# Feed-forward by halves of 288 tokens, outputs turned by DMA, products in token order: a change to a fused attention and feed-forward kernel

## Chip, cores and metric

The kernel runs on one core of one Trainium2 chip. The metric is the device time of one execution in microseconds (us), lower is better. Runs are compared in the same state of the chip and beside runs of the kernel before on the same chip; a run over 1.5% above the fastest of its kernel is called slow and left out of the ratios. "Span" is the time from the first to the last instruction in a profile; it is some 1.8 us shorter than the device time (256.4 against 258.15 us in the profile before).

## The reference

Eight batches of 576 tokens, eight heads of 64 channels. Heads 0 to 3 ("plain") look back over 32 tokens, heads 4 to 7 ("dilated") over 32 tokens in steps of 4. The concatenated heads go through a multiplicative feed-forward.

```python
def _attn_ref(q, k, v):                       # (8, 8, 576, 64)
    scores = scale * np.matmul(q, k.transpose(0, 1, 3, 2))
    rel = pos[:, None] - pos[None, :]
    mask_plain = (rel >= 0) & (rel < 32)
    mask_dil = (rel >= 0) & (rel < 128) & (rel % 4 == 0)
    ...                                       # softmax under the head's mask
    return np.matmul(attn, v)

def _moe_ref(x, w1, w2, w3, w_out):           # x: (4608, 512)
    h = (x @ w1) * (x @ w2) @ w3              # 1024 wide
    return h @ w_out                          # (4608, 512)
```

## The kernel before

TensorE does everything in one stream: `w3 @ w_out` is fused once into `wf_sb`; then each tile of 512 tokens gets its gated products (`ffn1`: two matrices of four matmuls of 512 columns per 128 of the 1024 channels, the first cast by ScalarE, the product by VectorE) and four results `y` (`ffn2`). The attention of later batches is put between these at counted "points". A batch's attention has four steps: two dilated halves (u = 1), then two plain halves (u = 0). A step is: scores (TensorE), exp (ScalarE), mask (VectorE), values (TensorE), reciprocal and normalise into `xo` (VectorE), and a turn of `xo` into channels, `XT`. In the kernel before, the turn is done on TensorE, but for the dilated halves of late batches, which a DMA turns.

```python
# self.by_dma = u == 1 and b > 1 and (b, hf) != (2, 1)
def to_channels(self, ps=ps_x, copy=None):
    if self.by_dma:
        for hp in range(2):
            nc.sync.dma_start(out=XT[:, 2 + hp, t0 : t0 + HALF]..., in_=self.xo[0:96, hp]..., transpose=True)
        return
    ...                       # six turns on TensorE into PSUM, one copy into XT

def ffn1(t, f, point):
    for i, w_sb in enumerate((w1_sb, w2_sb)):
        point()
        ps = bank()                                  # three banks in turn
        ffn1_half(t, f, w_sb, (2, 3, 0, 1), ps)      # four matmuls, 512 columns
        if i == 0: nc.scalar.copy(out=a_sb, in_=ps)
    nc.vector.tensor_tensor(out=gts[t][:, f], in0=pss[1], in1=a_sb, op=AL.mult)

for t in range(1, NT):
    for f in range(KFF): ffn1(t, f, point)
    for tb in range(4):  ffn2(t, tb, point)          # rows stored with a step of 4
```

Tokens stand in `XT` sorted by their number modulo 4, so `ffn2` stores rows with a step of four. Loads of q, k and v are issued by GpSimd two batches ahead, each as soon as its buffer is free.

The softmax here doesn't subtract the row's maximum and nothing guards it: scores larger than these inputs give would overflow.

Of the kernel before, what the change touches and what calls it, by code (L numbers as in the profile page):

```python
# [1 line left out]

# [29 lines left out]

SLOTS = (0, 2, 1, 3)


@with_exitstack
def kernel(
# [46 lines left out]
    XT = const.tile([P, DCH, n_tok], BF16, name="XT")  # L84
# [20 lines left out]
    def bank():  # L105
        return banks.tile([P, TB], F32, tag="f", name="f")
# [125 lines left out]
    def transpose_qk(b, u, which):  # L232


        src, dst = ((qn, qts), (kn, kts))[which]
        pad = PADK * which
        t = src[b][:, u, :].bitcast(U32).rearrange("p (a i) -> p a i", a=ROWS)
        o = dst[u][b % 2].rearrange("p s c -> p (s c)").bitcast(U32)[:, pad : pad + S]
        if u == 0 and which == 1:
            nc.vector.transpose(out=o.rearrange("p (j a) -> p a j", a=ROWS), in_=t)  # L240
            return
        for a0 in range(4):

            n = 5 - a0 // 2
            at = RES * SLOTS.index(a0)
            step = RES * SLOTS.index((a0 + 2) % 4) + (a0 + 18) // 4 - at
            nc.vector.transpose(  # L247
                out=bass.AP(
                    tensor=o.tensor,
                    offset=o.offset + at,  # L250
                    ap=[o.ap[0], [1, n], [9, 16], [step, 2]],
                ),
                in_=t[:, a0 : a0 + 4 * n - 3 : 4, :],
            )

    class Step:
        def __init__(self, n, b, u, hf):
            self.b, self.u, self.hf = b, u, hf
            self.et = ets[n % NET]

            self.by_dma = u == 1 and b > 1 and (b, hf) != (2, 1)
# [106 lines left out]
        def to_channels(self, ps=ps_x, copy=None):  # L368
            if self.by_dma:
                for hp in range(2):  # L370
                    t0 = self.b * S + HALF * self.hf
                    nc.sync.dma_start(
                        out=XT[:, 2 + hp, t0 : t0 + HALF].rearrange("p (m t) -> p m t", m=3),
# [4 lines left out]
            xv = ps[:, 0 : 2 * HALF].rearrange("p (h s t) -> p h s t", h=2, s=4)  # L378
            for hp in range(2):
                for m in range(3):  # L380
                    if self.u == 0:
                        xo = xv[:, hp, :, 24 * m : 24 * m + 24]
                    else:
                        xo = xv[:, hp].rearrange("p s t -> p (s t)")[:, 96 * m : 96 * m + 96]
                    nc.tensor.transpose(  # L385
                        out=xo,
# [3 lines left out]
            dst = XT[:, 2 * self.u : 2 * self.u + 2, self.b * S : (self.b + 1) * S]  # L390
            if self.u == 0:
                t0 = 72 * self.hf
                dst = dst.rearrange("p h (s t) -> p h s t", s=4)[:, :, :, t0 : t0 + 72]
            else:
                t0 = HALF * self.hf
                dst = dst[:, :, t0 : t0 + HALF].rearrange("p h (s t) -> p h s t", s=4)
            if copy is None:
                copy = nc.vector.tensor_copy if self.u == 0 and self.b > 1 else nc.scalar.copy
# [29 lines left out]
    def first_batch():  # L428
# [22 lines left out]
        ps_b = [pool.tile([P, TB], F32, name=f"ps_b{i}") for i in range(4)]  # L451
        begin(0, 0, ps_b[0])
        begin(0, 1, ps_b[1])
        p0.to_channels()
        begin(1, 0, ps_b[2])
        p1.to_channels(bank().bitcast(BF16), nc.vector.tensor_copy)
        begin(1, 1, ps_b[3])
# [33 lines left out]
    def segment(lo, hi):  # L491

        for i in range(lo, hi + 2):
            st = steps[i] if i < hi else None
            p1 = steps[i - 1] if lo <= i - 1 < hi else None
            p2 = steps[i - 2] if lo <= i - 2 else None
            at, b = i % 4, i // 4
            more = 4 * (b + 1) < hi and st is not None
            if st is not None:
                later(st.scores, after=1.0 if p2 is not None and not p2.by_dma else 1.6)  # L500
            if p2 is not None and not p2.by_dma:
                later(p2.to_channels)
                done_at[i - 2] = len(phases)
            if p1 is not None:
                later(p1.values, after=1.6)
                if p1.by_dma:
                    behind(p1.to_channels)
            if st is not None:
                if at == 0:
                    behind(transpose_qk, b, 0, 1)  # L510
                if at == 1:
                    if more:
                        behind(transpose_qk, b + 1, 1, 0)
                if at == 2:
                    behind(prefetch, b + 2)
                if at == 2 and more:
                    behind(transpose_qk, b + 1, 1, 1)
                if at == 3 and more:
                    behind(transpose_qk, b + 1, 0, 0)
# [5 lines left out]
    gts = {}  # L525

    def ffn1_half(t, f, w_sb, cs, ps):
        for c in cs:
            nc.tensor.matmul(  # L529
                out=ps,  # L530
                lhsT=w_sb[:, c, f * P : (f + 1) * P],
                rhs=XT[:, c, t * TB : (t + 1) * TB],
# [6 lines left out]
    def begin(f, i, ps):  # L539

        begun[f, i] = ps
        ffn1_half(0, f, (w1_sb, w2_sb)[i], (2, 3), begun[f, i])

    def ffn1(t, f, point):
        if t not in gts:
            gts[t] = wk_pool.tile([P, KFF, TB], BF16, tag="gt", bufs=3, name="gt")
        pss = []
        for i, w_sb in enumerate((w1_sb, w2_sb)):
            point()
# [168 lines left out]
```

## Time and profile before

| | before |
|---|---|
| time, median of 3 runs | 258.35 us (258.26 to 259.26) |
| span of the profile | 256.4 us |
| TensorE busy | 246.9 us (96%) |
| VectorE, ScalarE busy | 154.7, 111.2 us |
| turns on TensorE, turning DMAs | 126, 22 |

The page gives the busy time of each engine and the chain of work that ended last. The table of windows gives busy times by stretch, so that one sees where an engine idles. The groups give count, mean duration and what the engine waited for. The lines themselves stand in the prediction below, with what is to be seen in them.

### The profile page before, as it was taken

The page shows a single profiled execution, that of the slowest core. Times are in us where ns is not written, and L with a number is a line of the kernel's source. Part 1 is how long each engine was busy: PE and PEld are TensorE (multiplying, and loading weights), DVE is VectorE, ACT ScalarE, POOL GpSimd, SP SyncE. Part 2 cuts the span into 40 slices and gives each one's busy share as a digit, 9 for nine tenths or more (in the row PEclk, how much of TensorE's full clock was granted, in tenths as well). Part 3 has the DMA queues.
Part 4 walks back from the last instruction along what each step waited for, and adds up shares of the span by engine and source line. Part 5 has one row for each costly group of instructions (what it writes and reads, how often), then busy time and mean ns, then how long its engine had stood idle before and what let it go on. Part 6 is the DMA issues. An engine that isn't in the chain of part 4 may idle for free.

```text
span 256.4 us, 5585 instructions
## 1 busy us (share of the span) xinstructions
PE 246.9 (96%) x2281; PEld 124.7 (49%) x2318; DVE 154.7 (60%) x326; ACT 111.2 (43%) x161; POOL 57.7 (23%) x84
## 2 busy tenths in 40 slices
PE   7899999999999999999999999999999999999994
PEld 2454455655445544554455454545544544444443
DVE  6565445968897688848775777588746623412420
ACT  2444266554554454444445444444354224324232
POOL 8962235537261123114210600000000000000000
PEclk9999999999999999999999999999999999999999
DMA  6999999999999999686969791220142031014004
GB/s 102 167 189 208 207 212 200 190 197 213 247 188 176 211 201 139 96 157 149 115 107 211 107 92 42 98 76 3 48 100 66 0 92 74 0 51 113 3 27 137
DMA packets 59001, 32.12 MB, mean 125 GB/s; under 512 B 45024, under 2 KB 49376, under 8 KB 58976
## 3 DMA queue, kind: packets, MB, share of 16 engines
q0 software_dynamic: 46160, 20.70, 67.4%
q1 hardware_dynamic: 12816, 11.07, 15.8%
q8 instruction: 18, 0.29, 0.5%
q14 instruction: 7, 0.06, 0.1%
HBM read 41.39 MB, written 9.44 MB: 198 GB/s over the span
## 4 chain that ended last, share of the span: by engine, by line
PE 90%; DVE 3%; DMA 2%; issue 2%; ACT 1%; POOL 0%; POOLq 0%; ACTq 0%
PE f L529 45%; PE f L585 24%; PE f L615 5%; PE ps_a L319 4%; PE ps_a L277 4%; DMA kn<-in_k_dram 2%; PE ps_x L385 2%; PE ps_b L529 1%; PE f L601 1%; PE ps_s L277 1%; PE ps_s L293 1%; PE ps_x L179 1%; DVE xo L330 1%; DVE kt L240 0%; DVE gt L560 0%
## 5 line engine op out<-in xcount | busy, mean ns | idle before, releaser
L529 PE MATMUL f<-XT,w_sb 128*128 128x512 bf16 x537 | 127.0, 379 | 1.5 <-issue 0.5
L529 PEld LDWEIGHTS <-w_sb 128*128 128x128 bf16 x576 | 53.3, 98 | 60.2 <-DVE XT L399 0.6
L560 DVE TENSOR_TENSOR gt<-f,asb 128x512 bf16<-128x512 f32 x70 | 48.1, 687 | 38.5 <-PE f L529 37.8
L559 ACT CAST asb<-f 128x512 bf16<-128x512 f32 x70 | 41.0, 586 | 63.7 <-PE f L529 63.7
L585 PE MATMUL f<-wf_sb,gt 128*128 128x512 bf16 (+1 forms) x288 | 66.0, 373 | 1.0 <-issue 0.8
L592 ACT COPY osb<-f 128x512 f32<-128x512 f32 (+1 forms) x37 | 21.2, 574 | 47.5 <-PE f L585 47.2
L585 PEld LDWEIGHTS <-gt 128*128 128x128 bf16 x296 | 27.1, 98 | 27.9 <-DVE gt L560 0.5
L307 ACT ACTIVATE et<-ps_a 128x1152 bf16<-128x1152 f32 x28 | 31.7, 1134 | 7.9 <-PE ps_a L277 7.9
L140 POOL DMA_DIRECT2D vd<-in_v_dram x32 | 21.2, 668 | 39.8 <-PE ps_a L319 31.4
L330 DVE TENSOR_TENSOR xo<-ps_a,rcp 96x768 bf16<-96x768 f32 x28 | 26.7, 953 | 1.0
L247 DVE STREAM_TRANSPOSE qt<-qn 128x160 uint32<-128x160 uint32 (+1 forms) x64 | 19.6, 421 | 1.1 <-DMA qn<-in_q_dram 1.1
L308 DVE TENSOR_TENSOR et<-et,mask_di 128x1152 bf16<-128x1152 bf16 x14 | 10.6, 756 | 15.2 <-ACT et L307 15.2
L319 PEld LDWEIGHTS <-et 128*128 128x128 bf16 x384 | 15.8, 98 | 7.2 <-ACT et L297 0.6
L308 DVE TENSOR_TENSOR et<-et,mask_pl 128x1152 bf16<-128x1152 bf16 x14 | 10.6, 758 | 12.2 <-ACT et L307 12.0
L277 PEld LDWEIGHTS <-kt 32*128 32x128 bf16 x768 | 10.7, 92 | 14.7 <-issue 12.2
L615 PE MATMUL f<-wo_sb,w3T 128*128 128x512 bf16 x60 | 15.6, 379 | 0.2
L327 DVE RECIPROCAL rcp<-ps_a 96x12 f32<-96x12 f32 x28 | 6.2, 221 | 11.1 <-PE ps_a L319 11.0
L277 PE MATMUL ps_a<-qt,kt 32*128 32x96 bf16 x672 | 12.4, 202 | 0.1
L116 POOL DMA_DIRECT2D kn<-in_k_dram x10 | 6.4, 642 | 22.2 <-DVE kt L240 18.2
L116 POOL DMA_DIRECT2D qn<-in_q_dram x10 | 6.6, 662 | 18.8 <-DVE qt L247 15.3
L247 DVE STREAM_TRANSPOSE kt<-kn 128x160 uint32<-128x160 uint32 (+1 forms) x32 | 9.7, 416 | 1.6 <-DMA kn<-in_k_dram 1.5
L297 ACT ACTIVATE et<-ps_s 128x576 bf16<-128x576 f32 x8 | 5.2, 651 | 11.9 <-PE ps_s L277 11.6
(60 smaller groups left out, 142.9 us busy)
## 6 DMA issues: line engine op xcount, KB each, us to landing
qn<-in_q_dram POOLq DMA_DIRECT2D x6, 576.0 KB, 5.6
kn<-in_k_dram POOLq DMA_DIRECT2D x6, 576.0 KB, 9.4
w3n<-in_moe_w_dram POOLq DMA_DIRECT2D x4, 512.0 KB, 17.8
vp<-in_v_dram POOLq DMA_DIRECT2D x5, 384.0 KB, 7.0
out_dram<-osb SPq DMA_DIRECT2D x7, 256.0 KB, 2.3
out_dram<-osb SPq DMA_DIRECT2D x8, 224.0 KB, 2.3
out_dram<-osb SPq DMA_DIRECT2D x8, 192.0 KB, 3.0
out_dram<-osb SPq DMA_DIRECT2D x8, 160.0 KB, 3.0
```

Of the source, the lines that this page charges most:

```text
L140: nc.gpsimd.dma_start(out=vds[b % 2][p0 : p0 + n, 4 * m : 4 * m + 4, 16 : 16 + 2 * D], in_=bass.AP(tensor=x.tensor, offset=x.offset + (4 * ...
L247: nc.vector.transpose(out=bass.AP(tensor=o.tensor, offset=o.offset + at, ap=[o.ap[0], [1, n], [9, 16], [step, 2]],), in_=t[:, a0 : a0 + 4 ...
L277: nc.tensor.matmul(out=bank_of(h)[:, c0 : c0 + 96], lhsT=kt[prt, 96 * m : 96 * m + P, c], rhs=rhs, start=(start and c == 0), stop=(c == 1 ...
L307: nc.scalar.activation(out=ev, in_=ps_a[:, :, 0:HALF], func=ACT.Exp, scale=scale)
L308: nc.vector.tensor_tensor(out=ev, in0=ev, in1=mk.unsqueeze(1).to_broadcast([P, 4, HALF]), op=AL.mult)
L319: nc.tensor.matmul(out=out, lhsT=self.et[:, c0 : c0 + P], rhs=rhs, start=True, stop=True)
L330: nc.vector.tensor_tensor(out=xo[0:96].rearrange("p (n k) d -> p n k d", n=n), in0=ov[0:96, :, :, x0 : x0 + D], in1=rcp[0:96].unsqueeze(3) ...
L529: nc.tensor.matmul(out=ps, lhsT=w_sb[:, c, f * P : (f + 1) * P], rhs=XT[:, c, t * TB : (t + 1) * TB], start=(c == 2), stop=(c == 1),)
L559: nc.scalar.copy(out=a_sb, in_=ps)
L560: nc.vector.tensor_tensor(out=gts[t][:, f], in0=pss[1], in1=a_sb, op=AL.mult)
L585: nc.tensor.matmul(out=y, lhsT=gts[t][:, f, tb * P : (tb + 1) * P], rhs=wf_sb[:, f, c0 : c0 + n], start=(f == 0), stop=(f == KFF - 1),)
L615: nc.tensor.matmul(out=wf_ps[ft], lhsT=w3T[ft][:, g, :], rhs=wo_sb[:, g, :], start=(g == 0), stop=(g == KFF - 1),)
```

## The change

Its intent: turns cost TensorE time (43 ns each in the profile before, 126 of them), so from batch 2 on a DMA does them all. The feed-forward goes by halves of a batch (288 tokens), and results `y` of the half before are put between its products, to give ScalarE and VectorE time. Products are written to `gt` in token order, so that each tile of 128 tokens goes out in one plain store. A fourth PSUM bank (`ps_x`) joins the ring after batch 1; VectorE's turns of q and k are cut into pieces and spread.

```diff
-            self.by_dma = u == 1 and b > 1 and (b, hf) != (2, 1)
+            self.by_dma = b > 1
@@ bank()
+        if "x" in late:
+            late["x"] += 1
+            if late["x"] % 4 == 0:
+                return ps_x.bitcast(F32)
@@ ffn1
-        nc.vector.tensor_tensor(out=gts[t][:, f], in0=pss[1], in1=a_sb, op=AL.mult)
+        n0 = HALF * (2 * b + hf) % RING
+        g = gt[:, f, n0 : n0 + HALF].rearrange("p (i a c) -> p c a i", a=2, c=2)
+        pb, pa = (
+            x.rearrange("p (c a i) -> p c a i", c=2, a=2) for x in (pss[1], a_sb)
+        )
+        nc.vector.tensor_tensor(out=g, in0=pb, in1=pa, op=AL.mult)
@@ schedule
-    for t in range(2, 8):
-        marks.append((15 + 24 * t, done_at[4 * t + 3]))
+    for b in range(2, B):
+        marks.append((40 + 27.25 * (b - 1) - 4, done_at[4 * b + 3]))
@@ main loop
+    done, due = len(due), []
+    for b in range(1, B):
+        for hf in range(2):
+            for f in range(KFF):
+                ffn1(b, hf, f, point)
+                if due and f in (1, 3, 5):
+                    ffn2(due.pop(0), point)
+            while P * (done + 1) <= b * S + (hf + 1) * HALF:
+                due.append(done)
+                done += 1
+        if b == 1:
+            late["x"] = 0
+    for t in due:
+        ffn2(t, point)
... (first batch, segment(), store() and layouts cut)
```

More of the change, by code (lines that the diff above doesn't have):

```diff
@@ L1 @@
 from contextlib import ExitStack
+from functools import partial
 import numpy as np
@@ L33 @@
 SLOTS = (0, 2, 1, 3)
+RING = 4 * HALF
 @with_exitstack
@@ L83 @@
     wf_sb = const.tile([P, KFF, d_model], BF16, name="wf_sb")
-    XT = const.tile([P, DCH, n_tok], BF16, name="XT")
+    XT = [const.tile([P, 2, n_tok], BF16, name=f"XT{u}") for u in range(2)]
+    gt = const.tile([P, KFF, RING], BF16, name="gt")
     ident = const.tile([P, P], BF16, name="ident")
@@ L229, in const_masks, with transposes, piece @@
             )
-    def transpose_qk(b, u, which):
+    def transposes(b, u, which):
         src, dst = ((qn, qts), (kn, kts))[which]
         pad = PADK * which
-        t = src[b][:, u, :].bitcast(U32).rearrange("p (a i) -> p a i", a=ROWS)
-        o = dst[u][b % 2].rearrange("p s c -> p (s c)").bitcast(U32)[:, pad : pad + S]
-        if u == 0 and which == 1:
-            nc.vector.transpose(out=o.rearrange("p (j a) -> p a j", a=ROWS), in_=t)
-            return
-        for a0 in range(4):
-            n = 5 - a0 // 2
-            at = RES * SLOTS.index(a0)
-            step = RES * SLOTS.index((a0 + 2) % 4) + (a0 + 18) // 4 - at
+        def piece(k):
+            t = src[b][:, u, :].bitcast(U32).rearrange("p (a i) -> p a i", a=ROWS)
+            o = dst[u][b % 2].rearrange("p s c -> p (s c)").bitcast(U32)[:, pad : pad + S]
+            if u == 0 and which == 1:
+                a = slice(9 * k, 9 * k + 9)
+                nc.vector.transpose(
+                    out=o.rearrange("p (j a) -> p a j", a=ROWS)[:, a], in_=t[:, a]
+                )
+                return
+            n = 5 - k // 2
+            at = RES * SLOTS.index(k)
+            step = RES * SLOTS.index((k + 2) % 4) + (k + 18) // 4 - at
             nc.vector.transpose(
@@ L252, in transpose_qk @@
                 ),
-                in_=t[:, a0 : a0 + 4 * n - 3 : 4, :],
+                in_=t[:, k : k + 4 * n - 3 : 4, :],
             )
+        return [partial(piece, k) for k in range(2 if u == 0 and which == 1 else 4)]
+    def transpose_qk(b, u, which):
+        for f in transposes(b, u, which):
+            f()
     class Step:
@@ L366, in values, with to_channels @@
             self.normalize(ov, self.xo.rearrange("p h j d -> p (h j) d"), 4, 3)()
-        def to_channels(self, ps=ps_x, copy=None):
+        def to_channels(self, ps=ps_x, copy=nc.scalar.copy):
+            t0 = self.b * S + HALF * self.hf
+            dst = XT[self.u][:, :, t0 : t0 + HALF]
             if self.by_dma:
                 for hp in range(2):
-                    t0 = self.b * S + HALF * self.hf
                     nc.sync.dma_start(
-                        out=XT[:, 2 + hp, t0 : t0 + HALF].rearrange("p (m t) -> p m t", m=3),
+                        out=dst[:, hp].rearrange("p (m t) -> p m t", m=3),
                         in_=self.xo[0:96, hp].rearrange("p (m h) d -> p m (h d)", m=3),
@@ L377, in to_channels @@
                 return
-            xv = ps[:, 0 : 2 * HALF].rearrange("p (h s t) -> p h s t", h=2, s=4)
+            xv = ps[:, 0 : 2 * HALF].rearrange("p (h x) -> p h x", h=2)
             for hp in range(2):
                 for m in range(3):
-                    if self.u == 0:
-                        xo = xv[:, hp, :, 24 * m : 24 * m + 24]
-                    else:
-                        xo = xv[:, hp].rearrange("p s t -> p (s t)")[:, 96 * m : 96 * m + 96]
                     nc.tensor.transpose(
-                        out=xo,
+                        out=xv[:, hp, 96 * m : 96 * m + 96],
                         in_=self.xo[0:96, hp, 2 * m : 2 * m + 2, :],
@@ L389, in to_channels @@
                     )
-            dst = XT[:, 2 * self.u : 2 * self.u + 2, self.b * S : (self.b + 1) * S]
-            if self.u == 0:
-                t0 = 72 * self.hf
-                dst = dst.rearrange("p h (s t) -> p h s t", s=4)[:, :, :, t0 : t0 + 72]
-            else:
-                t0 = HALF * self.hf
-                dst = dst[:, :, t0 : t0 + HALF].rearrange("p h (s t) -> p h s t", s=4)
-            if copy is None:
-                copy = nc.vector.tensor_copy if self.u == 0 and self.b > 1 else nc.scalar.copy
             copy(out=dst, in_=xv)
@@ L451, in first_batch @@
         ps_b = [pool.tile([P, TB], F32, name=f"ps_b{i}") for i in range(4)]
+        late.update(b=ps_b, n=0)
         begin(0, 0, ps_b[0])
@@ L455, in first_batch @@
         begin(1, 0, ps_b[2])
+        begin(1, 1, ps_b[3])
+        ffn1(0, 0, 0)
         p1.to_channels(bank().bitcast(BF16), nc.vector.tensor_copy)
-        begin(1, 1, ps_b[3])
         const_masks()
@@ L491, in segment @@
     def segment(lo, hi):
-        for i in range(lo, hi + 2):
-            st = steps[i] if i < hi else None
-            p1 = steps[i - 1] if lo <= i - 1 < hi else None
-            p2 = steps[i - 2] if lo <= i - 2 else None
-            at, b = i % 4, i // 4
-            more = 4 * (b + 1) < hi and st is not None
-            if st is not None:
-                later(st.scores, after=1.0 if p2 is not None and not p2.by_dma else 1.6)
-            if p2 is not None and not p2.by_dma:
-                later(p2.to_channels)
-                done_at[i - 2] = len(phases)
-            if p1 is not None:
-                later(p1.values, after=1.6)
-                if p1.by_dma:
-                    behind(p1.to_channels)
-            if st is not None:
-                if at == 0:
-                    behind(transpose_qk, b, 0, 1)
-                if at == 1:
-                    if more:
-                        behind(transpose_qk, b + 1, 1, 0)
-                if at == 2:
-                    behind(prefetch, b + 2)
-                if at == 2 and more:
-                    behind(transpose_qk, b + 1, 1, 1)
-                if at == 3 and more:
-                    behind(transpose_qk, b + 1, 0, 0)
@@ new lines, in segment, with some @@
+        pieces = []
+        def some():
+            for f in pieces[:2]:
+                behind(f)
+            del pieces[:2]
+        for i in range(lo, hi + 1):
+            at, b = i % 4, i // 4
+            more = 4 * (b + 1) < hi
+            if at == 0 and i < hi:
+                pieces += transposes(b, 0, 1)
+                for u, which in ((1, 0), (1, 1), (0, 0)) if more else ():
+                    pieces += transposes(b + 1, u, which)
+            if i < hi:
+                later(steps[i].scores, after=0.8)
+                later(lambda: None, after=0.8)
+                some()
+            if i > lo:
+                later(steps[i - 1].values, after=0.8)
+                behind(steps[i - 1].to_channels)
+                done_at[i - 1] = len(phases)
+                if i < hi:
+                    later(lambda: None, after=0.8)
+                    some()
+            if at == 2:
+                behind(prefetch, b + 2)
@@ L521, with ffn1_half @@
     second_batch()
     segment(8, 4 * B)
-    gts = {}
-    def ffn1_half(t, f, w_sb, cs, ps):
+    def ffn1_half(b, hf, f, w_sb, cs, ps):
         for c in cs:
+            x = XT[c // 2][:, c % 2, b * S : (b + 1) * S]
+            if c < 2:
+                x = x[:, HALF * hf : HALF * hf + HALF]
+                x = x.rearrange("p (m s j) -> p s m j", m=3, s=4)
+            else:
+                n = HALF // 4
+                x = x.rearrange("p (s i) -> p s i", s=4)[:, :, n * hf : n * hf + n]
@@ L529, in ffn1_half @@
             nc.tensor.matmul(
-                out=ps,
+                out=ps[:, 0:HALF],
                 lhsT=w_sb[:, c, f * P : (f + 1) * P],
-                rhs=XT[:, c, t * TB : (t + 1) * TB],
+                rhs=x,
                 start=(c == 2),
@@ L541, in begin, with ffn1 @@
         begun[f, i] = ps
-        ffn1_half(0, f, (w1_sb, w2_sb)[i], (2, 3), begun[f, i])
-    def ffn1(t, f, point):
-        if t not in gts:
-            gts[t] = wk_pool.tile([P, KFF, TB], BF16, tag="gt", bufs=3, name="gt")
+        ffn1_half(0, 0, f, (w1_sb, w2_sb)[i], (2, 3), ps)
+    def ffn1(b, hf, f, point=None):
         pss = []
         for i, w_sb in enumerate((w1_sb, w2_sb)):
-            point()
-            if t == 0 and (f, i) in begun:
-                ps = begun[f, i]
-                ffn1_half(t, f, w_sb, (0, 1), ps)
-            else:
-                ps = bank()
-                ffn1_half(t, f, w_sb, (2, 3, 0, 1), ps)
-            pss.append(ps)
-            if len(pss) == 1:
-                a_sb = wk_pool.tile([P, TB], BF16, tag="asb", bufs=3, name="asb")
-                nc.scalar.copy(out=a_sb, in_=ps)
-        nc.vector.tensor_tensor(out=gts[t][:, f], in0=pss[1], in1=a_sb, op=AL.mult)
@@ L562, in store @@
-    def store(o_sb, r0, cols):
-        n = 0
-        while n < P:
-            b, p = divmod(r0 + n, S)
-            slot, i = divmod(p, RES)
-            m = min(P - n, RES - i)
-            row = b * S + 4 * i + SLOTS[slot]
-            nc.sync.dma_start(
-                out=out[row : row + 4 * (m - 1) + 1 : 4, cols], in_=o_sb[n : n + m, cols]
-            )
-            n += m
-    def ffn2(t, tb, point):
-        last = t == NT - 1 and tb == 3
+            if point is not None:
+                point(0.57)
@@ new lines, in ffn1 @@
+            if (b, hf) == (0, 0) and (f, i) in begun:
+                ps, cs = begun[f, i], (0, 1)
+            else:
+                if b == 0:
+                    ps = late["b"][late["n"] % 4]
+                    late["n"] += 1
+                else:
+                    ps = bank()
+                cs = (2, 3, 0, 1)
+            ffn1_half(b, hf, f, w_sb, cs, ps)
+            pss.append(ps[:, 0:HALF])
+            if len(pss) == 1:
+                a_sb = wk_pool.tile([P, HALF], BF16, tag="asb", bufs=3, name="asb")
+                nc.scalar.copy(out=a_sb, in_=pss[0])
@@ L578, in ffn2 @@
+        n0 = HALF * (2 * b + hf) % RING
+        g = gt[:, f, n0 : n0 + HALF].rearrange("p (i a c) -> p c a i", a=2, c=2)
+        pb, pa = (
+            x.rearrange("p (c a i) -> p c a i", c=2, a=2) for x in (pss[1], a_sb)
+        )
+        nc.vector.tensor_tensor(out=g, in0=pb, in1=pa, op=AL.mult)
+    def ffn2(t, point):
+        last = t == n_tok // P - 1
         o_sb = wk_pool.tile([P, d_model], F32, tag="osb", bufs=6, name="osb")
+        n0 = t * P % RING
         for c0, n in ((0, 256), (256, 256)) if last else ((0, 512),):
-            point()
+            point(1)
@@ L583, in ffn2 @@
                 if f == KFF // 2 and not last:
-                    point()
+                    point(1)
                 nc.tensor.matmul(
                     out=y,
-                    lhsT=gts[t][:, f, tb * P : (tb + 1) * P],
+                    lhsT=gt[:, f, n0 : n0 + P],
                     rhs=wf_sb[:, f, c0 : c0 + n],
@@ L592, in ffn2 @@
             nc.scalar.copy(out=o_sb[:, c0 : c0 + n], in_=y)
-            store(o_sb, t * TB + tb * P, slice(c0, c0 + n))
+            nc.sync.dma_start(
+                out=out[t * P : (t + 1) * P, c0 : c0 + n], in_=o_sb[:, c0 : c0 + n]
+            )
     w3T = {}
@@ L655, with point @@
     marks = [(40, n0)]
-    for t in range(2, 8):
-        marks.append((15 + 24 * t, done_at[4 * t + 3]))
+    for b in range(2, B):
+        marks.append((40 + 27.25 * (b - 1) - 4, done_at[4 * b + 3]))
     place = np.concatenate([[0.0], np.cumsum(room)])
     xs, ys = [m[0] for m in marks], [place[m[1]] for m in marks]
-    def point():
-        state[0] += 1
+    def point(n):
+        state[0] += n
         want = int(np.searchsorted(place, np.interp(state[0], xs, ys) - 1e-6))
@@ L667, in point @@
             state[1] += 1
-    for f in range(KFF):
-        if f == KFF - 1:
+    for f in range(1, KFF + 2):
+        if f < KFF:
+            ffn1(0, 0, f)
+        if f == KFF:
             fuse_t(0)
-        ffn1(0, f, point)
+        if f >= 2:
+            ffn1(0, 1, f - 2)
+    state[0] = 2 * KFF
     late["a"] = four_banks().tile([P, 4, TB], F32, name="ps_a")
@@ L677 @@
         for half in range(2):
-            point()
+            point(1)
             fuse_m(ft, half)
-    for tb in range(4):
-        ffn2(0, tb, point)
-    for t in range(1, NT):
-        for f in range(KFF):
-            ffn1(t, f, point)
-        for tb in range(4):
-            ffn2(t, tb, point)
+    due = list(range(S // P))
+    for t in due:
[12 more added lines that the diff above has]
+            late["x"] = 0
+    for t in due:
+        ffn2(t, point)
     assert state[1] == len(phases)
```

## The prediction

Passages without a measurement of this case behind them are cut and marked. No term of the sum is among them: it came to 258.0 us, shaded to 257.4. The one part of the argument that goes with them is the support for taking the strided write as free; what is left of it is an assumption. Where the text after the first cut says "they", the matmuls of 128 columns are meant, 8 in 0.61 us beside 8 loads (profile before, from 34.80 us). The 2.4 columns per ns are the slope of the measured spacings, (215.5 - 56) / (512 - 128) = 0.415 ns a column. The hand-over of 0.25 us is the distance from the start of the last of six turns (20.59 + 5 x 0.043 = 20.80 us) to the start of its copy (21.05).

> **What bounds the kernel now.** I read the page's first part, its slices and its chain, then the table of windows, the groups by shape, the timeline of single stretches, and the landings of the turning DMAs. The page, then four windows of the table (length, then busy time of PE, PEld, DVE, ACT, POOL with counts, clock, DMA share, GB/s):
>
> ```profile
> PE 246.9 (96%) x2281; PEld 124.7 (49%) x2318; DVE 154.7 (60%) x326; ACT 111.2 (43%) x161; POOL 57.7 (23%) x84
> PE 90%; DVE 3%; DMA 2%; issue 2%; ACT 1%; POOL 0%; POOLq 0%; ACTq 0%
> ```
> ```profile
> 0.00:6.40 6.40, 4.94 (x12) 1.79 (x13) 4.05 (x30) 1.28 (x1) 5.15 (x15) 1.00 0.61 102
> 6.40:20.00 13.60, 11.90 (x185) 6.95 (x186) 8.37 (x26) 5.74 (x9) 11.16 (x16) 1.00 1.58 180
> ...
> 125.00:150.00 25.00, 24.68 (x251) 12.37 (x254) 18.11 (x38) 11.15 (x16) 5.47 (x7) 1.00 1.04 138
> ...
> 250.00:256.40 6.40, 3.00 (x22) 1.96 (x20) 0.00 (x0) 1.48 (x4) 0.00 (x0) 1.00 0.43 136
> ```
>
> The reader is to see that TensorE leaves 9.5 us of a span of 256.4 idle, and that 6.6 of those lie before 20 us and after 250 us (1.46 + 1.70 + 3.40). Between, it is busy 24.68 us of 25. Busy is a union of modelled ends, so I checked that the stream is dense as well. Spacing comes from runs in the timeline: 12 feed-forward matmuls of 512 columns take 2.75 us in one run; less the last one's own 379 ns that is 2371/11 = 215.5 ns apart. Eight of 128 columns take 0.61 us, (610-219)/7 = 56 ns. The last token tile's y is done in pieces of 256 columns, 16 in 1.9 us, (1900-272)/15 = 109 ns. Six turns of 96 columns take 0.42 us, (420-205)/5 = 43 ns. All fit columns/2.4 GHz + 2 to 3 ns. So TensorE is bound by the columns that it streams, not by weights or waits.
>
> [...] here they stand 56 ns apart, each with its own load, so a load does not bound a matmul of 288 columns. [...] The products in token order are written at a step of 4 bf16 elements, 8 bytes[...]; the new moving operand has runs of 24 elements, 48 bytes. The kernel before has no such write, so no run here shows it; it does read queries in runs of 24 for the plain heads, and those 24 score matmuls take 0.45 us against 0.44 for the dilated ones. I charge nothing for either. [...]
>
> **The change, part by part.** The groups that size it (line, engine, operation, tiles, shapes, count, then busy us and mean ns, then idle before):
>
> ```profile
> L560 DVE TENSOR_TENSOR gt<-f,asb 128x512 bf16<-128x512 f32 x70 | 48.1, 687 | 38.5 <-PE f L529 37.8
> L559 ACT CAST asb<-f 128x512 bf16<-128x512 f32 x70 | 41.0, 586 | 63.7 <-PE f L529 63.7
> L592 ACT COPY osb<-f 128x256 f32<-128x256 f32 x2 | 0.7, 373 | 0.8 <-PE f L585 0.5 <-DMA out_dram<-osb 0.3
> L385 PEld LDWEIGHTS <-xo 96*128 96x128 bf16 x126 | 7.5, 97 | 4.6
> L399 DVE COPY XT<-ps_x 128x576 bf16<-128x576 bf16 x13 | 5.9, 454 | 3.8 <-PE ps_x L385 3.8
> L293 PE MATMUL ps_s<-neg_di,ident 128*128 128x288 bf16 x8 | 1.6, 287 | 0.0
> ```
>
> Halves: 9 tiles x 8 x 2 x 4 = 576 matmuls of 512 columns become 16 x 64 = 1024 of 288, the same 294,912 columns. 576 x 215.5 = 124.1 us become 1024 x 122.4 (288/2.4 + 2.4) = 125.3. **+1.2 us** on TensorE. The 287 ns of one 288-column matmul against 379 confirms the slope: 92 ns for 224 columns.
>
> Turns by DMA: 126 turns stand on TensorE (the loads count them). Batches 0 and 1 keep 8 x 6 = 48; 78 go. 78 x 43 ns = **-3.35 us**, all on the path, for PE has no slack. y, fuse, scores and values are unchanged. TensorE's sum is therefore -2.15 us.
>
> VectorE: 72 products of 687 ns (49.5) become 128. A fit through 512 and the copy-like cost of the 768-wide normalise (953 ns) gives 1.04 ns a column + 154, so 454 ns for 288: 58.1. +8.6. Gone are 12 copies of 454: -5.4; split key turns add about 1. It comes to some 159 us of 256, no bound on average. ScalarE: 586 and 373 ns give 0.83 a column, 399 at 288; 128 x 399 = 51.1 against 42.2: +8.9, no bound at 47%.
>
> First batch: four products' begun halves shrink from 8 x 215 to 8 x 122 ns, so less covers the first plain output's copy (639 ns on ScalarE plus some 0.25 us of hand-over), which now stands behind only the 0.49 us of the last two begun halves. I estimate **+0.5 us**. The end is alike: a split last tile, one copy, one store. y between products and a fourth bank remove no wait, for there is none in the middle to remove; they are to keep one from arising. Single stores per tile spare SP issues that are hidden already.
>
> **Rivals.** First, **banks**. A bank filled by 512 columns takes 0.86 us, so with three banks a product may lag its last matmul by 2 x 0.86 = 1.73 us. With 288 columns a bank takes 0.49; four banks allow 3 x 0.49 = 1.47, and batch 1, still on three, only 0.98. A y between adds 1.73. What lags cost is seen in the timeline of VectorE:
>
> ```profile
> 98.36 0.76 DVE L308 TENSOR_TENSOR et<-et,mask_pl 128x1152 bf16<-128x1152 bf16 x1 [1.11 <-ACT et L307]
> 99.03 1.46 DVE L560 TENSOR_TENSOR gt<-f,asb 128x512 bf16<-128x512 f32 x2
> 100.41 0.22 DVE L327 RECIPROCAL rcp<-ps_a 96x12 f32<-96x12 f32 x1
> 100.67 0.95 DVE L330 TENSOR_TENSOR xo<-ps_a,rcp 96x768 bf16<-96x768 f32 x1
> 101.54 1.22 DVE L247 STREAM_TRANSPOSE qt<-qn 128x160 uint32<-128x160 uint32 x4
> 102.61 0.67 DVE L560 TENSOR_TENSOR gt<-f,asb 128x512 bf16<-128x512 f32 x1
> ```
>
> The mask waits 1.11 us for exp and two products queue behind it; reciprocal, normalise and turns (2.4 us) hold up the next. The change splits the turns in twos (about 0.85 us) and spreads them, which speaks for it; the tighter ring speaks against. A mask ahead of a product delays it to about 1.7 us after its matmul, 0.2 to 0.4 us too late where no y is near. Over 28 steps, a third of them in such a place, this is 1 to 3 us, plus 1 to 3 in batch 1. If masks and turns always fell beside a y it would be 0. I take 1 us, since the dummy phases and the fourth bank look made for it.
>
> Second, **landings**. The turning DMAs of one step, by stretch of time, first 60 to 75 us, then 93 to 96:
>
> ```profile
> DMA to landing us min/median/max: 9.4/9.8/10.3
> ```
> ```profile
> DMA to landing us min/median/max: 5.3/5.3/5.3
> ```
>
> They are slow while the loads fill the queues (DMA share over 1.2 until 100 us). Now batch 2's plain outputs go this way too. Its first plain half is issued some 10.8 points (about 11 us) before its products need it; after 2 to 3 us on VectorE and 2.5 us for two issues of 1.24 us, 5 to 6 us are left. A landing of 10 us would cost up to 4 us, once. Later batches have landings of 2.3 to 6 and are safe. I take 0.3 us.
>
> Third, **VectorE as the bound** in stretches without y: in 6.9 us, 3.6 of attention and six products of 0.454 are 92% plus waits. This would add to the first rival and reach 264 at the worst.
>
> **Range and chances.** 258.35 - 3.35 + 1.2 + 0.5 + 1.0 + 0.3 = 258.0. The change looks tuned to avoid the two rivals, so I shade it to **257.4 us**. If neither arises, 255.7; with single stalls at both, 262. Range 254.4 to 262.0. Faster by 2% needs 253.2, more than all the turns give: 0.04. Slower by 2% (263.5) needs both rivals in full: 0.08. Within 2%: 0.88.
>
> **What would show it.** Right: 48 turns left on TensorE, its matmuls of 288 some 122 ns apart, PE busy about 2 us less, products near 454 ns, 46 to 48 turning DMAs on SP. Wrong: idle time before the feed-forward matmuls released by VectorE's products or ScalarE's casts (first rival), most of it between 62 and 90 us; by a DMA into XT near 88 us (second); or a spacing over 122 ns in the products of plain heads, which would mean that strided operands cost something. Products well over 454 ns would tell of the strided write.

## The result

The changed kernel takes 266.08 us (median of 4 runs, 265.93 to 270.5) against 258.81 us for the kernel before in the same group: ratio 1.0286, 95% interval 1.0238 to 1.0333. It is slower by nearly 3%, outside the range. All ratios here are of mean times of fast runs from the same rounds, so not quite the ratio of the medians that I quote.

The lines below come from the changed kernel run again (run a1_after, span 264.6 us). Its page and windows, to be read against the same lines of before:

```profile
PE 249.0 (94%) x2658; PEld 165.5 (63%) x2688; DVE 192.7 (73%) x378; ACT 118.0 (45%) x216; POOL 57.8 (22%) x84
PE 80%; DVE 5%; DMA 5%; issue 4%; ACT 2%; POOL 2%; SPq 0%; POOLq 0%; DVEq 0%; ACTq 0%
```
```profile
6.40:20.00 13.60, 11.75 (x195) 7.40 (x195) 9.43 (x29) 5.83 (x10) 11.00 (x16) 1.00 1.57 179
...
80.00:100.00 20.00, 16.58 (x184) 10.68 (x185) 14.37 (x28) 8.11 (x15) 3.77 (x5) 0.91 1.36 148
...
125.00:150.00 25.00, 24.45 (x291) 16.99 (x292) 20.04 (x37) 12.24 (x23) 5.49 (x7) 1.00 0.96 131
```

In the kernel before, the stretch from 80 to 100 us reads:

```profile
80.00:100.00 20.00, 19.68 (x205) 9.98 (x209) 14.64 (x30) 9.62 (x14) 5.47 (x7) 1.00 1.44 185
```

TensorE's share of the chain fell from 90 to 80%; VectorE and DMA now have 5% each, where they had 3 and 2%. VectorE's busy time rose by 38 us. Between 80 and 100 us TensorE is busy 16.58 us where it had been 19.68 before, and its granted clock there is 0.91 (a share of full speed). The groups by shape and the waits of TensorE (total, times, longest):

```profile
L584 DVE TENSOR_TENSOR gt<-f,asb 128x288 bf16<-128x288 f32 x91 | 71.2, 804 | 15.6 <-PE f L544 15.3
L577 ACT CAST asb<-f 128x288 bf16<-128x288 f32 x85 | 34.0, 400 | 41.5 <-PE f L544 38.5 <-DVE qt L261 2.1 <-DVE gt L584 0.6
L401 PEld LDWEIGHTS <-xo 96*128 96x128 bf16 x48 | 2.8, 97 | 1.2
```
```profile
PE f L544 <- DMA XT<-xo: 3.3, 1, 3.3
PE f L544 <- DVE gt L584: 2.1, 4, 0.8
...
PE ps_x L544 <- DVE gt L584: 0.9, 2, 0.6
```

The turns left are 48 and the cast takes 400 ns, both as worked out. The product takes 804 ns, not 454. TensorE waits for two things that it never waited for before: a turning DMA (3.3 us, once) and products of VectorE (3.0 us, six times). The place of the first, in the timelines of VectorE, SP and TensorE:

```profile
83.91 0.81 DVE L584 TENSOR_TENSOR gt<-f,asb 128x288 bf16<-128x288 f32 x1
84.52 0.21 DVE L346 RECIPROCAL rcp<-ps_a 96x12 f32<-96x12 f32 x1
84.78 0.95 DVE L349 TENSOR_TENSOR xo<-ps_a,rcp 96x768 bf16<-96x768 f32 x1
```
```profile
85.77 2.47 SPq L392 DMA_TRANSPOSE XT<-xo  x2
```
```profile
89.03 0.53 PE L338 MATMUL ps_a<-vp,et 128*128 128x65 bf16 x12
89.40 1.02 PE L544 MATMUL f<-XT,w_sb 128*128 128x288 bf16 x7
93.69 1.98 PE L544 MATMUL f<-XT,w_sb 128*128 128x288 bf16 x9 [3.27 <-DMA XT<-xo]
```
```profile
DMA to landing us min/median/max: 4.3/5.5/6.7
```

The values of batch 2's first plain half were done at 83.4 us. `xo` came at 85.73, behind turns of q and a product; the two DMAs were issued at 85.8 and 87.0 and landed 4.3 and 6.7 us later (last line: this step's landings), the second at 93.6. TensorE wanted it at 90.4. The batch's last values (89.03) are computed just as its products begin. Soon after that wait of 3.27 us the clock is down. This is the window in question (from `prof a1_after --windows 94.08:97.49`):

```profile
94.08:97.49 3.41, 3.41 (x37) 1.89 (x35) 1.56 (x2) 0.94 (x3) 0.00 (x0) 0.50 0.94 184
```

For 3.41 us TensorE runs at half speed, and its matmuls of 288 columns begin 240 ns apart instead of 122. That is 1.7 us lost. The first profile shows the same: 3.41 us at 0.50 from 95.17 us on, after a wait of 3.45 us. Not every wait is followed by it: after one of 2.50 us in the first profile, at 124.1 us, the clock stays at 1.00.

For a ledger I summed, over all neighbouring matmuls of one line with 288 or 512 columns, what their start-to-start distance exceeds columns/2.4 + 2.5 ns ("excess"; the line fits the spacings before, 109 ns at 256 columns and 215.5 at 512; where a record is missing, two or three distances are allowed). It is 1.0 us before and 10.4 in a1_after: 4.2 of it between 80 and 100 us, 1.6 between 60 and 80 (batch 1, three banks), 0.8 between 20 and 40 against 0.3 before (first batch), and most of the rest in single waits of 0.3 to 1.0 us for products. A spacing of 240 ns at half speed counts in it as one missing record, so what the clock loses is not in these sums.

### The profile page after: what moved, and what is told of

Same layout as the page of the kernel before. It is cut to its first block, busy times and chain, and to the rows that moved or that the text cites. A ratio compares the mean times of both kernels' runs of the same rounds, so it can differ in the third digit from the quotient of the medians.

```text
span 268.7 us, 6577 instructions
## 1 busy us (share of the span) xinstructions
PE 249.6 (93%) x2658; PEld 165.4 (62%) x2688; DVE 193.1 (72%) x378; ACT 118.0 (44%) x216; POOL 57.8 (22%) x84
## 4 chain that ended last, share of the span: by engine, by line
PE 71%; DMA 14%; POOL 4%; DVE 4%; issue 3%; ACT 1%; SPq 0%; POOLq 0%; DVEq 0%
PE f L544 26%; PE f L598 17%; DMA XT<-xo 9%; PE ps_x L544 8%; DMA w_sb<-in_moe_w_dram 5%; PE f L630 5%; PE ps_x L598 4%; PE ps_b L544 4%; PE ps_a L338 3%; PE ps_a L296 3%; DVE gt L584 2%; POOL w_sb L161 1%; ACT et L326 1%; PE f L616 1%; POOL vd L150 1%
## 5 line engine op out<-in xcount | busy, mean ns | idle before, releaser
L544 PEld LDWEIGHTS <-w_sb 128*128 128x128 bf16 x1024 | 97.3, 98 | 44.4 <-issue 13.7
L544 PE MATMUL f<-XT,w_sb 128*128 128x288 bf16 x704 | 102.2, 287 | 9.2 <-DMA XT<-xo 7.3
L584 DVE TENSOR_TENSOR gt<-f,asb 128x288 bf16<-128x288 f32 x91 | 71.3, 803 | 17.9 <-PE f L544 17.4
L598 PE MATMUL f<-wf_sb,gt 128*128 128x512 bf16 (+1 forms) x222 | 54.1, 372 | 1.3 <-issue 0.5
L577 ACT CAST asb<-f 128x288 bf16<-128x288 f32 x85 | 34.0, 400 | 45.5 <-PE f L544 42.5
L544 PE MATMUL ps_x<-XT,w_sb 128*128 128x288 bf16 x192 | 31.9, 289 | 0.9 <-DVE gt L584 0.9
L584 DVE TENSOR_TENSOR gt<-ps_x,asb 128x288 bf16<-128x288 f32 x21 | 16.9, 803 | 3.9 <-PE ps_x L544 3.6
L544 PE MATMUL ps_b<-XT,w_sb 128*128 128x288 bf16 x128 | 17.1, 286 | 1.3 <-DMA w_sb<-in_moe_w_dram 0.6
L296 PEld LDWEIGHTS <-kt 32*128 32x128 bf16 x768 | 10.8, 94 | 11.7 <-issue 9.0
L584 DVE TENSOR_TENSOR gt<-ps_b,asb 128x288 bf16<-128x288 f32 x16 | 12.6, 806 | 5.4 <-PE f L401 2.3
L577 ACT CAST asb<-ps_x 128x288 bf16<-128x288 f32 x27 | 10.8, 400 | 12.8 <-PE ps_x L544 11.3
L598 PE MATMUL ps_x<-wf_sb,gt 128*128 128x512 bf16 x50 | 12.9, 379 | 0.4 <-issue 0.2
```

The costliest lines, as they stand in the source:

```text
L296: nc.tensor.matmul(out=bank_of(h)[:, c0 : c0 + 96], lhsT=kt[prt, 96 * m : 96 * m + P, c], rhs=rhs, start=(start and c == 0), stop=(c == 1 ...
L544: nc.tensor.matmul(out=ps[:, 0:HALF], lhsT=w_sb[:, c, f * P : (f + 1) * P], rhs=x, start=(c == 2), stop=(c == 1),)
L577: nc.scalar.copy(out=a_sb, in_=pss[0])
L584: nc.vector.tensor_tensor(out=g, in0=pb, in1=pa, op=AL.mult)
L598: nc.tensor.matmul(out=y, lhsT=gt[:, f, n0 : n0 + P], rhs=wf_sb[:, f, c0 : c0 + n], start=(f == 0), stop=(f == KFF - 1),)
```

## The experiments

Theory A: the strided write makes products slow, VectorE falls behind and holds banks and late outputs. Theory B: the turning DMAs of the plain halves land too late beside the loads, whatever VectorE does. In each group the kernel before ran too. Edits are against the changed kernel.

**a1_after**: no edit, the control.

> The changed kernel again, as the control of this group: some 266 us. In a run of the fast state the turning DMAs of batches 2 to 4 should still hold up the feed-forward by 2 to 7 us in sum, and the products should take about 803 ns.

Measured: 267.13 us, ratio 1.0377 (1.0346 to 1.0408). Its runs lie between 266.4 and 268.5, with clocks of 0.987 to 0.994.

**a2_contig**: products contiguous, order put right by the stores.

```diff
-        g = gt[:, f, n0 : n0 + HALF].rearrange("p (i a c) -> p c a i", a=2, c=2)
-        ...                                          # the views pb and pa
-        nc.vector.tensor_tensor(out=g, in0=pb, in1=pa, op=AL.mult)
+        nc.vector.tensor_tensor(out=gt[:, f, n0 : n0 + HALF], in0=pss[1], in1=a_sb, op=AL.mult)
...
-            nc.sync.dma_start(out=out[t * P : (t + 1) * P, ...], in_=o_sb[...])
+            store(o_sb, t * P, slice(c0, c0 + n))    # pieces, rows with a step of 4
```

> Products written in the order of the products before them, without the step of four elements; rows put in token order by the stores instead. Theory A (the strided write costs 350 ns per product, VectorE falls behind, the normalised outputs and so the turning DMAs come late): products about 454 ns, VectorE busy down by some 44 us, the waits for the turning DMAs down to under 3 us, time 258 to 261 us. Theory B (the landings are too slow whatever VectorE does): products also 454 ns, but the waits for the turning DMAs stay at 5 us or more, time 263 to 265 us.

Measured: 265.61 us, ratio 1.0295 (1.0278 to 1.0312). Its profile is read for durations and for who waits for whom:

```profile
L581 DVE TENSOR_TENSOR gt<-f,asb 128x288 bf16<-128x288 f32 x91 | 40.7, 452 | 32.1 <-PE f L544 31.8
```
```profile
PE f L544 <- DMA XT<-xo: 6.2, 4, 2.2
```

Contiguous, the same product takes 452 ns, and the waits for products are down to 0.2 us. But the waits for turning DMAs are 6.2 us. A alone would have given 258 to 261; the time was above even what B expected, by less than 1 us. Its fast runs also have a lower clock than the control's, in the mean 0.985 against 0.992: by estimate 0.007 x 264 = some 1.8 us more are lost to the lower clock. One thing is mixed in: the edit also cuts each store into pieces, which go out on the same queue as the turning DMAs. e4_step2 below has whole stores and products of 478 ns, and TensorE still waits 4.1 us for turning DMAs (263.25 us in its one run). So a faster VectorE alone does not remove these waits; how much of the 6.2 us is due to the pieces was not tested.

**a3_early**: `40 + 27.25 * (b - 1) - 4` becomes `- 9`.

> Only the schedule of the attention is moved 5 points (some 5 us) earlier against the feed-forward, products strided as in the change. Theory B: the waits for turning DMAs go to under 1 us and the time to 258 to 260 us, for VectorE is busy but not the bound. Theory A in its strong form (VectorE so loaded that it holds banks): the waits for DMAs go, but waits for products take their place, above all in batch 1 with three banks: 261 to 264 us.

Measured: 262.51 us, ratio 1.0184 (1.0169 to 1.02). No wait for a turning DMA is left in its trace, and waits for products (3.8 us in sum) remain, the mixed outcome foreseen under A. It also shows a flaw of the change: marks and loop disagree. The marks count 27.25 points per batch, but in batch 1 only the second half has `y` to put in, two tiles of two points, so it has 16 x 1.14 + 4 = 22.2 points and batch 2 begins 5 points earlier than its mark assumes.

**a4_contig_early**: both edits.

> Both of these edits. If strided products and late landings are the whole of the loss, TensorE's sum rules: 256 to 257.5 us, about 2 us under the kernel before. If banks of 288 columns cost something by themselves, 258 to 260 us with waits for products or casts left.

Measured: 266.97 us, ratio 1.0338 (1.031 to 1.0366). This contradicted me. Timelines of SP, GpSimd and TensorE:

```profile
76.89 7.87 SPq L392 DMA_TRANSPOSE XT<-xo  x4
```
```profile
82.24 0.70 POOL L126 DMA_DIRECT2D qn<-in_q_dram  x1 [2.95 <-DVE gt L581]
85.70 0.70 POOL L126 DMA_DIRECT2D kn<-in_k_dram  x1 [2.76 <-DVE rcp L346]
```
```profile
94.71 0.28 PE L544 MATMUL f<-XT,w_sb 128*128 128x288 bf16 x1 [3.62 <-DMA XT<-xo]
```

The fourth of these DMAs was issued by 84.8 us at the latest and TensorE got its data at 94.7: 10 us or more. The load of q, 576 KB, begins at 82.24 in the midst of them; in a3_early it begins at 83.60. My reading is that an earlier issue does not help when the load moves with it. That is argued, not shown: the stores in pieces are a rival here too. Between 80 and 100 us the DMA engines are busy for a share of 1.77 with 152 GB/s in this run, and of 1.44 with 167 GB/s in a3_early.

**c1_noload**: loads for batches 4 to 7 left out, older data used; wrong result.

```diff
+            if b >= 4:
+                qn[b], kn[b] = qn[b - 2], kn[b - 2]
+                return
             load_qk(b)
             load_vd(b)
```

> The changed kernel without the loads of q, k and v for batches 4 to 7 (older batches' data are used, so the result is wrong on purpose); all instructions of the engines stay. If the loads are what makes the turning DMAs of batches 2 and 3 land late: landings of 2.3 to 3.5 us from some 80 us on, no wait for a turning DMA left, time 261.5 to 263.5 us, the rest being waits for products. If the turning DMAs are slow by themselves, or their issue on SP is: landings stay at 5 us and more, time 265 us or more.

Measured: 261.74 us, ratio 1.0143 (1.0126 to 1.016). The same step's landings, then TensorE's window:

```profile
DMA to landing us min/median/max: 2.4/2.7/3.0
```
```profile
80.00:100.00 20.00, 19.51 (x244) 13.08 (x246) 16.99 (x34) 10.00 (x19) 0.00 (x0) 1.00 0.23 67
```

Landings fall from 4.3 to 6.7 us to 2.4 to 3.0, nothing waits for a turning DMA, and the clock stays at 1.00. The loads' presence costs the change 4 to 6 us (ratio 1.0143 against 1.0286 in the first group and 1.0377 in the control's). Waits for products stay: 3.6 us.

**c2_pe4**: plain outputs of batches 2 to 4 turned on TensorE, two phases after their values, copied by ScalarE.

```diff
-            self.by_dma = b > 1
+            self.by_dma = b > 4 or (b > 1 and u == 1)
+    def turn(st):
+        st.to_channels(ps_x if st.b == 2 else bank().bitcast(BF16))
```

> The plain outputs of batches 2, 3 and 4 are turned on TensorE again (36 turns, 1.5 us) and copied by ScalarE; the rest as in the change, products strided. If late landings of these outputs are the largest loss: waits for turning DMAs under 0.5 us, time 262 to 264 us. If the landings only hide a wait for VectorE behind them: waits for products grow in their place and the time stays at 265 us or more.

Measured: 265.89 us, ratio 1.0298 (1.0283 to 1.0314), a miss. Turning DMAs are waited for only once, for 0.2 us, but TensorE stands 1.6 us in front of one turn (released by a product, VectorE being behind), and 36 turns cost 1.5 us (by estimate, at 43 ns each). Waits for products are 3.4 us beside that, against 3.6 in c1_noload. Its time fits the second branch of the expectation, but the turn's own wait is new with this edit, so it does not decide between the theories; c1_noload and e1_hold do. I did not find the rest of the 4 us between this and c1_noload.

**b1_readperm**: token order by strided reads, contiguous write.

```diff
+        g = gt[:, f, n0 : n0 + HALF].rearrange("p (i a c) -> p i a c", a=2, c=2)
+        pb, pa = (x.rearrange("p (c a i) -> p i a c", c=2, a=2) for x in (pss[1], a_sb))
```

> Products in token order as in the change, but the permutation is in the reads (PSUM at a step of 72 words, the cast tile at a step of 144 bytes) and the write is contiguous; single stores stay. If only the strided write costs: about 454 ns per product and VectorE 36 us less busy. If strided reads cost as much: 800 ns or more. In time little by itself, 264.5 to 267 us, since the wait for the turning DMAs stays.

Measured: 265.50 us, ratio 1.0251 (1.0183 to 1.0318), so the verdict is unclear; the fast runs spread from 262.8 to 266.6 (a fourth, of 267.1, is of the slow state). The spread goes with the clock: 262.76 us at 1.000, 264.43 at 0.994, 266.56 at 0.992.

```profile
L584 DVE TENSOR_TENSOR gt<-f,asb 128x288 bf16<-128x288 f32 x91 | 55.9, 620 | 21.2 <-PE f L544 20.9
```

A product takes 620 ns, between the two forecasts. Strided reads cost too, but less than the strided write (620 ns against 804; contiguous 452). TensorE waits 5.3 us for turning DMAs.

**c4_pe4_bank1**: c2_pe4 with the fourth bank from batch 1 on (`late["x"] = 0` ahead of the loop).

> As c2, with the fourth bank from batch 1 on instead of batch 2. If three banks of 288 columns are what holds the feed-forward up around 65 to 80 us (0.83 us in one wait, 1.6 us in sum): these waits fall under 0.5 us and the time is 0.7 to 1.5 us below that of c2. If VectorE's backlog rules them, no difference.

Measured: 263.80 us, ratio 1.0226 (1.0209 to 1.0243), 2 us below c2_pe4, more than expected. Excess between 60 and 80 us falls only from 1.6 to 1.3; the 1.6 us wait for a turn became two of 0.75 and 0.95.

**d1_noload_contig**: c1_noload and a2_contig together; wrong result.

> Without the loads for batches 4 to 7 (wrong result on purpose, as before) and with contiguous products. If the waits of 0.6 to 1.0 us that stay without the loads are VectorE's backlog of strided products (804 ns): they go, but for those of batch 1 with three banks, and the time is 257.5 to 259 us. If halves of 288 columns hold banks up whatever a product costs: 260 us or more.

Measured: 257.86 us, ratio 0.998 (0.9947 to 1.0013). With both causes gone, the whole loss is gone. What halves of 288 columns cost by themselves is small: excess is 2.8 us against 1.0 before, and 1.0 of it lies between 60 and 80 us, in batch 1 with its three banks.

**d2_pre3, d3_contig_pre3_bank1, d4_best**: the call that issues loads moved by one step (`if at == 2` becomes `if at == 3`); d3 adds contiguous products and the fourth bank; d4 adds one more pair begun in the first batch and marks 2 points earlier.

> One edit to the change: the loads of a later batch are issued one step later, behind the turning DMAs of the first plain half instead of ahead of them. If the loads ahead in the queues are what makes these land late: landings of these under 4 us, waits for turning DMAs under 1 us, 261.5 to 263.5 us, like the run without loads. If total traffic matters and not the order: waits of 3 us or more stay, 265 us or more.

> Contiguous products, loads one step later, fourth bank from batch 1 on. All three losses taken away: 256.5 to 258.5 us, what is left being the first batch (0.8 us). If turning DMAs still wait: 260 us or more.

> As the last, with the products of one more pair begun in the first batch and the attention 2 points earlier: meant to beat the kernel before, 255.5 to 257.5 us. If the first batch waits for a copy or for weights anyway: as the last.

Measured: 267.91, 267.21 and 265.82 us; ratios 1.0378, 1.0339 and 1.0294. All three missed. In d2_pre3 the q load is still issued at the same moment:

```profile
86.36 0.70 POOL L126 DMA_DIRECT2D qn<-in_q_dram  x1 [4.23 <-DVE qt L261]
```

In a1_after that line reads 86.60, though the call was moved by one step (6 to 7 us). In both runs GpSimd stood idle for 4.23 us before the load, until VectorE had turned the q that stood in its buffer: it was ahead of the program's schedule, and the load went when the buffer was free. Moving the call moved nothing. d2 is therefore no test of the order of loads and turning DMAs. In d3 and d4, with contiguous products and stores in pieces again, single waits for turning DMAs reach 3.2 and 3.0 us (7.4 and 5.2 us in sum), and the runs' clocks are 0.983 to 0.985.

**e1_hold**: GpSimd first reads eight columns of the turned half, then issues the loads after it.

```diff
+    def hold(b):
+        t = b * S + HALF
+        nc.gpsimd.tensor_copy(out=held, in_=XT[0][:, 1, t - 8 : t])
+        if b + 2 < B:
+            load_vd(b + 2); load_vp(b + 2)      # taken out of prefetch(b + 2)
...
                 behind(steps[i - 1].to_channels)
+                if (i - 1) % 4 == 2:
+                    behind(hold, (i - 1) // 4)
```

> One edit to the change: GpSimd reads eight columns of each batch's first turned plain half (one small copy) ahead of the next loads, so that the v loads of that batch and the q and k loads after it start only when that half has landed. All loads stay, the result is right. If loads in flight beside the turning DMAs are the cause of the late landings: first plain halves land within 3.5 us, waits for turning DMAs under 1 us, 261.5 to 263.5 us like the run without loads. If the wait only moves to the loads' users or to the second half: 265 us or more.

Measured: 261.70 us, ratio 1.0137 (1.012 to 1.0155), right result. GpSimd's timeline, then the step's landings:

```profile
89.27 0.18 POOL L431 COPY held<-XT 128x8 bf16<-128x8 bf16 x1 [19.48 <-DMA XT<-xo]
89.78 2.64 POOL L150 DMA_DIRECT2D vd<-in_v_dram  x4 [0.34 <-PE f L556]
```
```profile
DMA to landing us min/median/max: 2.5/2.9/3.4
```

All loads are there, only later, and it equals the run without them (261.74). So it is loads in flight beside the turning DMAs, not their mere amount, that makes these land late. Which of the loads does it was not taken apart.

**e2_contig_hold**: the same with contiguous products.

> The same with contiguous products: both causes taken away, result right. 257.5 to 259 us, as in the run without loads and with contiguous products (257.86).

Measured: 258.28 us, ratio 1.0001 (0.9983 to 1.002), right result. The strided products cost 1.4% (1.0137 to 1.0001), and both causes together are the loss. Excess is 2.8 us.

**e3_best**: e2 with the fourth bank from batch 1, one more pair begun, marks 2 points earlier.

> The same with the fourth bank from batch 1, one more pair begun in the first batch and the attention 2 points earlier. If TensorE's sum then rules: 255.5 to 257 us, under the kernel before by 0.5 to 1 per cent.

Measured: 257.64 us, ratio 0.998 (0.9958 to 1.0001): less than hoped. The pair begun in the first batch waits 0.73 us for its weights, and the earlier schedule brings two waits of 0.33 us at 118 and 172 us.

**e4_step2**: products at a step of 2 elements; wrong order on purpose, one look.

```diff
-  .rearrange("p (i a c) -> p c a i", a=2, c=2)
+  .rearrange("p (c i a) -> p c a i", a=2, c=2)
```

> One look, wrong order on purpose: products of the change written at a step of two elements (4 bytes) instead of four (8 bytes). If the cost goes with the bytes between neighbours: between 452 and 804 ns, some 550 to 650. If any step costs the same: 804 ns.

Measured: 478 ns per product (263.25 us, one run, state unknown).

```profile
L584 DVE TENSOR_TENSOR gt<-f,asb 128x288 bf16<-128x288 f32 x91 | 43.0, 478 | 27.1 <-PE f L544 26.8
```

The cost is not in proportion to the step: 452 ns at 2 bytes between neighbours, 478 at 4, 804 at 8.

**f1_bank1, f2_dvecopy**: e2 with the fourth bank from batch 1; f2 also copies the first batch's first plain half on VectorE.

> Contiguous products, loads held until the first turned plain half has landed, fourth bank from batch 1; schedule and first batch as in the change. The waits of e2 between 60 and 80 us (1.0 us) should go, those of e3 near 118 and 172 us should not come: 257.0 to 257.6 us, under the kernel before by 0.2 to 0.4 per cent.

> The same with the first batch's first plain half copied by VectorE instead of ScalarE (459 against 640 ns): the wait of 0.4 us near 20 us shrinks by some 0.2 us, or nothing changes if VectorE is busy there. 256.9 to 257.6 us.

Measured: 257.05 us, ratio 0.9969 (0.995 to 0.9989), and 257.16 us, ratio 0.9967 (0.9951 to 0.9983), right results. Both beat the kernel before, by 0.3%, with intervals that leave out 1; f2's copy is worth nothing that can be told from f1. The ledger of f1: excess 2.6 us, 1.6 more than before; taken from the 2.15 us that TensorE saves, it leaves 0.55 us of gain, against some 0.8 measured.

## Why the prediction was wrong

**Right.** TensorE's sum: 48 turns are left, and eight matmuls of 288 columns take 1.14 us in the first profile, (1140 - 286)/7 = 122 ns apart, as worked out; half of these eight read plain heads, in runs of 24 elements, so these strided operands cost nothing that shows. The cast at 400 ns and the first batch's extra 0.5 us (excess 0.8 against 0.3) came as estimated. A contiguous product takes 452 ns, against 454 estimated. Both rivals that happened were named, with the signs that would tell of them. One sign was misplaced: most waits for products were to come between 62 and 90 us, but of the single excesses that they leave in a1_after only one (1.0 us, at 68.7) lies there, and five of 0.4 to 0.7 us lie between 147 and 207 us.

**The first step that failed: "I charge nothing for either."** The kernel before has no such write, as the prediction says, so that it is free was an assumption which no run of this case had shown. The product costs 804 ns instead of 454, 128 x 350 ns = 45 us of instruction time. VectorE's busy time, in which instructions can overlap (in a1_after the product at 82.70 us begins 0.08 us before the mask ahead of it ends), differs by 36 us (192.7 in a1_after, 156.6 in a2_contig). With it, the first rival, put at 1 us, was about 3.5 us: e1_hold to e2_contig_hold is 1.0137 to 1.0001. With contiguous products the ring of four banks is wide enough: in d1 and in e2 TensorE waits once for a product, 0.2 us. Batch 1's three banks cost another 0.3% (e2 to f1).

**The second: "Its first plain half is issued some 10.8 points (about 11 us) before its products need it."** I took the marks at their word. The loop runs 5 points ahead of them, since `y` lags by a half and batch 1 has only two to place. From values to first use it was 7.0 us (83.4 to 90.4), not 11; VectorE took 2.4 and the issues 2.5, as estimated, though part of that was strided products. What was left after both issues was 2.1 us, not 5 to 6. Counted from the start of the second issue it was 3.4 us, and that landing took 6.7.

**The third, a term mis-sized: "I take 0.3 us."** The wait was 3.3 us in a1_after and half speed followed it, worth another 1.7 us, which the prediction did not count. With and without it (a1_after against e1_hold) the ratios are 1.0377 and 1.0137; against the first group's 1.0286 it is 1.5%. So 4 to 6 us.

**Also wrong: "The change looks tuned to avoid the two rivals, so I shade it."** That is no evidence from the profile. The sum before shading was 258.0 and would have missed as well, but the worst case that I had worked out, 264, was left out of the range. The measured 266.08 lies above that too.

What stays open: why a turning DMA beside loads lands only after 4 to 10 us; what stores in pieces add to that; and the rest of the time of c2_pe4.

## What to carry to other kernels

Moving work off the bounding engine is worth what its sum says only if what replaces it arrives in time: here the sum said 2.15 us less, and one turning DMA held TensorE up for 3.3 us (a1_after). Work out the lead from the loop as it runs, not from the schedule's own constants, and take the landing time from a stretch with the same transfers beside it: 4.3 to 6.7 us beside loads (a1_after), 2.4 to 3.0 without them (c1_noload). GpSimd, with only DMAs to issue there, ran ahead of the program: moving the call left the q load where it was (86.36 us in d2_pre3, 86.60 in a1_after), and giving the loads something to wait for moved them (89.78 us and later in e1_hold). A wait of TensorE can cost more than its own length: 3.41 us at half speed followed the one of 3.27 us in a1_after. Before using a strided write on a busy engine, look for that very step in a trace, or measure it: here a product took 452 ns at 2 bytes between neighbours, 478 at 4 and 804 at 8.
